# Loading attention keys in 8 KB rows, with transposes that sort two interleaved batches

## The chip, the cores and the metric

One core of one Trainium2 chip. Times are device microseconds of whole executions. The medians are of unprofiled runs; a profile is one more execution, a little shorter or longer. All profiled runs here are fast, with a mean granted TensorE clock of 0.98 to 0.99 of full speed. Ratios are the mean time of one kernel's fast runs over that of the kernel before in the same rounds, so not quite the ratio of the medians that are quoted beside them.

## The reference, cut to what matters

Two independent attention blocks A and B, bf16, whose outputs are put side by side:

```python
B, Sq, D = 16, 64, 640;  H, Sk, Dh = 32, 512, 128
q = (x @ wq).reshape(B, Sq, H, Dh).transpose(0, 2, 1, 3)
scores = einsum("bhqd,bhkd->bhqk", q, k_cache) * Dh ** -0.5
p = softmax(scores)
o = einsum("bhqk,bhkd->bhqd", p, v_cache)
out = o.transpose(0, 2, 1, 3).reshape(B, Sq, H * Dh) @ wo
```

The two K and two V caches are 67 MB each and every byte is used once, so 268 MB of the 295 MB moved are K and V.

## The kernel before

The work is cut into 128 **packs** of two batches and four heads. In each pack TensorE projects the queries (QP), computes the scores (S), transposes the probabilities (TR), multiplies them with V (PV) and applies `wo` (OP). ScalarE takes the exponentials (EX) with row sums. VectorE transposes K (KT), copies the transposed probabilities out of PSUM (TE), takes reciprocals of the row sums (RC) and, once in four packs, moves the output sum (OS). GpSimd scales the probabilities (NM). The kernel gives each engine one ordered list. The lists are sorted by planned times, in packs: `OS=2.53` of pack n-2 falls at the same time as the first RC, 0.53, of pack n, and stands ahead of it.

A pack's K arrives as two DMAs, one per batch, of 128 rows of 4 KB: partition 32·head + p holds 16 keys. VectorE then transposes blocks of 32 x 32 fp32 words (each word two bf16 values of one key), so that keys end up along the free dimension:

```python
def em_LDK(e, op):                      # one batch b of pack n
    src = blocks[blk][1][2 * bp + b, h:h + 4].rearrange("h (p t) d -> (h p) (t d)", t=16)
    ins = e.dma_start(kn_ring[:, n % NK, b, :], src)
...
def em_KT(e, op):
    dst = kt_ring[:, n % NKT, b].rearrange("p t j k two -> p (t j k two)").bitcast(F32)
    ins = e.transpose(dst, kn_ring[:, n % NK, b, :].bitcast(F32))
...
def em_S(e, op):                        # 32 matmuls a pack
    last = e.matmul(ps[64 * b:64 * b + 64, i, :], qs_ring[rows, n % NQ, f, b, :],
                    kt_ring[rows, n % NKT, b, :, f // 2, :, f % 2],
                    start=(f == 0), stop=(f == 3), tile_position=(32 * i, 64 * b))
...
def exp_views(h):                       # every fourth pack ("narrow") reorders keys for its V layout
    if h // 4 % NJ in WIDE:
        return src, dst
    return (src.rearrange("q (th tl k) -> q tl k th", th=2, tl=8), ...)
```

The rings hold six packs of K and four of V. SyncE issues the loads in a fixed order as slots become free.

## Time and profile before

| | before |
|---|---|
| median | 757.96 us (757.82 to 759.49, 3 runs) |
| span of the profiled run | 757.4 us |
| DMA | 295.12 MB, full in all slices but the first and the last two |
| TensorE busy | 90% (98% from 60 to 225 us and from 640 to 738 us) |
| VectorE busy | 71% |
| one transpose of 1024 columns | 1236 ns, 256 of them |
| score matmuls of a pack | 146.4 us / 128 = 1.14 us |

Read it in two steps. The slices show which resources are full on average, here DMA and nearly TensorE. The windows and the waits then show which one holds up the other in each stretch. The lines are in the prediction below. Two groups are needed for the comparison with the profile after (line, engine, operation, tiles, shapes, count; then busy us, mean ns; then idle time before them and what ended it):

```profile
L610 DVE STREAM_TRANSPOSE kt_ring<-kn_ring 128x1024 f32<-128x1024 f32 x256 | 313.6, 1236 | 105.8 <-DMA kn_ring<-in_B_k_cache_dram 70.3
...
L620 PE MATMUL ps<-kt_ring,qs_ring 32*64 32x512 bf16 x4096 | 146.4, 396 | 0.0
```

VectorE had 106 us of idle time ahead of its transposes, most of it waiting for keys to land.

### The profile page before, as it was taken

The numbers are of one execution on the slowest core, as the hardware profiler recorded it, in microseconds if no ns is written. First come the engines' busy times: TensorE is split into PE (matmuls) and PEld (weight loads), VectorE is DVE, ScalarE is ACT, GpSimd is POOL, SyncE is SP. The second block draws the span as 40 slices with busy tenths as digits, with TensorE's granted clock in tenths as the row PEclk, the third lists the DMA queues.
The fourth block names the chain that finished last, engine by engine and source line by source line (L and its number), as shares of the span: only waits on it lengthen the run. The fifth ranks groups of instructions, "written<-read, shape, count | busy, mean of one in ns | idle before, by whom it ended". The sixth has DMA issues, their size and how long they took to land.

```text
span 757.4 us, 57362 instructions
## 1 busy us (share of the span) xinstructions
PE 682.2 (90%) x26518; PEld 528.0 (70%) x26518; DVE 536.7 (71%) x818; ACT 519.6 (69%) x1559; POOL 404.6 (53%) x580
## 2 busy tenths in 40 slices
PE   4579999999999989999978999899997999999995
PEld 3457777777777767777756776677775777777773
DVE  7437777877767777687756777777675787887873
ACT  2437777777777677767756777777775677777772
POOL 5434555546864544645674455445486556455550
PEclk9979999999999999999999999999999999999997
DMA  8999999999999999999999999999999999999970
GB/s 309 394 399 405 406 406 407 406 405 407 400 395 409 407 408 406 407 407 407 406 394 401 406 407 407 406 405 405 406 403 395 406 408 407 402 409 406 407 294 16
DMA packets 99804, 295.12 MB, mean 390 GB/s; under 512 B 9264, under 2 KB 24112, under 8 KB 99760
## 3 DMA queue, kind: packets, MB, share of 16 engines
q1 hardware_dynamic: 91120, 284.20, 95.7%
q10 hardware_dynamic: 8640, 10.49, 3.8%
q14 instruction: 35, 0.29, 0.1%
q8 instruction: 9, 0.15, 0.1%
HBM read 292.03 MB, written 2.62 MB: 389 GB/s over the span
## 4 chain that ended last, share of the span: by engine, by line
PE 33%; SPq 26%; DMA 19%; POOL 9%; DVE 8%; issue 5%; ACT 0%; POOLq 0%; DVEq 0%; ACTq 0%
SPq L546 12%; POOL pn_sb L670 8%; SPq L557 8%; PE ps L705 8%; PE ps L725 8%; PE ps L597 7%; DMA kn_ring<-in_B_k_cache_dram 6%; PE ps L620 6%; DMA kn_ring<-in_A_k_cache_dram 5%; PE ps L681 5%; SPq L559 5%; DMA v_ring<-in_B_v_cache_dram 5%; DVE pT_sb L691 3%; DMA v_ring<-in_A_v_cache_dram 3%; DVE kt_ring L610 1%
## 5 line engine op out<-in xcount | busy, mean ns | idle before, releaser
L670 POOL TENSOR_SCALAR pn_sb<-p_ring,recip 128x512 bf16<-128x512 bf16 x508 | 342.3, 694 | 322.9 <-DVE recip L654 322.8
L610 DVE STREAM_TRANSPOSE kt_ring<-kn_ring 128x1024 f32<-128x1024 f32 x256 | 313.6, 1236 | 105.8 <-DMA kn_ring<-in_B_k_cache_dram 70.3
L641 ACT ACTIVATE p_ring<-ps 128x512 bf16<-128x512 f32 x512 | 298.7, 598 | 32.1 <-PE ps L620 20.3
L691 DVE COPY pT_sb<-ps 128x1024 bf16<-128x1024 bf16 x258 | 164.6, 679 | 79.5 <-PE ps L681 78.8
L705 PE MATMUL ps<-pT_sb,v_ring 32*128 32x64 bf16 (+1 forms) x14528 | 156.7, 192 | 26.2 <-DMA v_ring<-in_B_v_cache_dram 11.0
L725 PE MATMUL ps<-wo_sb,oT_sb 128*128 128x320 bf16 x1040 | 166.6, 303 | 5.9 <-issue 4.8
L597 PE MATMUL ps<-xT_ring,wqp_sb 128*128 128x128 bf16 x2560 | 166.0, 220 | 6.1 <-POOL xT_ring L586 5.8
L705 PEld LDWEIGHTS ps<-pT_sb,v_ring 32*128 32x128 bf16 (+1 forms) x14528 | 142.1, 92 | 40.6 <-DMA v_ring<-in_B_v_cache_dram 14.1
L597 PEld LDWEIGHTS ps<-xT_ring,wqp_sb 128*128 128x128 bf16 x2560 | 157.4, 114 | 13.0 <-issue 6.0
L713 ACT ACTIVATE oT_sb<-ps 128x256 bf16<-128x256 f32 x260 | 85.6, 381 | 107.0 <-PE ps L705 107.0
L620 PE MATMUL ps<-kt_ring,qs_ring 32*64 32x512 bf16 x4096 | 146.4, 396 | 0.0
L603 ACT ACTIVATE qs_ring<-ps 128x512 bf16<-128x512 f32 x128 | 76.5, 598 | 87.7 <-PE ps L597 87.6
L681 PEld LDWEIGHTS ps<-ident,pn_sb 64*128 64x128 bf16 x4128 | 70.8, 95 | 86.8 <-ACT ps L717 65.6
L725 PEld LDWEIGHTS ps<-wo_sb,oT_sb 128*128 128x128 bf16 x1040 | 91.9, 98 | 43.8 <-issue 5.4
L681 PE MATMUL ps<-ident,pn_sb 64*128 64x64 bf16 x4128 | 84.0, 191 | 26.4 <-POOL pn_sb L670 19.8
L641 ACT ACTIVATION_READ_ACCUMULATOR p_ring<-ps 128x1 f32 x512 | 105.9, 207 | 0.0
L620 PEld LDWEIGHTS ps<-kt_ring,qs_ring 32*64 32x64 bf16 x4096 | 55.1, 104 | 31.3 <-issue 0.5
L654 DVE RECIPROCAL recip<-rowsum 128x3 f32<-128x3 f32 (+1 forms) x256 | 36.1, 158 | 24.5 <-ACT p_ring L641 21.2
L717 ACT ACTIVATE ps<-zeros 128x256 f32<-128x256 bf16 x130 | 51.3, 395 | 0.0
L569 POOL COPY wqp_sb<-ws_sb 128x1280 bf16<-128x1280 bf16 x32 | 39.3, 1260 | 7.5 <-DMA ws_sb<-in_A_wq_dram 7.5
L586 POOL COPY xT_ring<-xs_sb 128x640 bf16<-128x640 bf16 x32 | 23.0, 720 | 3.6 <-PE ps L597 3.6
L576 PE MATMUL ps<-ident,xn_ring 128*128 128x128 bf16 x165 | 14.9, 222 | 4.7 <-DMA xn_ring<-in_A_x_dram 3.5
(26 smaller groups left out, 66.3 us busy)
## 6 DMA issues: line engine op xcount, KB each, us to landing
kn_ring<-in_A_k_cache_dram SPq DMA_DIRECT2D x128, 512.0 KB, 14.1
v_ring<-in_A_v_cache_dram SPq DMA_DIRECT2D x128, 512.0 KB, 13.0
kn_ring<-in_B_k_cache_dram SPq DMA_DIRECT2D x128, 512.0 KB, 15.1
v_ring<-in_B_v_cache_dram SPq DMA_DIRECT2D x128, 512.0 KB, 12.7
ws_sb<-in_B_wq_dram SPq DMA_DIRECT2D x10, 512.0 KB, 15.6
wo_sb<-in_B_wo_dram ACTq DMA_DIRECT2D x8, 640.0 KB, 10.9
ws_sb<-in_A_wq_dram SPq DMA_DIRECT2D x4, 640.0 KB, 10.1
wo_sb<-in_A_wo_dram SPq DMA_DIRECT2D x4, 640.0 KB, 12.5
```

What stands on the lines that cost most here:

```text
L546: ins = e.dma_start(kn_ring[:, n % NK, b, :], src)
L597: last = e.matmul(ps[:, 1, f * 128:(f + 1) * 128], w[:, kt, f, :], xT_ring[:, xs, kt, :], start=(kt == 0), stop=(kt == KT - 1))
L603: ins = e.activation(qs_ring[:, op.idx % NQ].rearrange("p f b q -> p (f b q)"), ps[:, 1, :], ACTF.Copy, scale=scale)
L610: ins = e.transpose(dst, kn_ring[:, n % NK, b, :].bitcast(F32))
L620: last = e.matmul(ps[64 * b:64 * b + 64, i, :], qs_ring[rows, n % NQ, f, b, :], kt_ring[rows, n % NKT, b, :, f // 2, :, f % 2], start=(f = ...
L641: ins = e.activation(dst, src, ACTF.Exp, scale=1.0, accum_out=rowsum[:, h:h + 1])
L670: ins = e.tensor_scalar(dst, src, recip[:, h // 4 % NR, i:i + 1], 1.0, ALU.mult, ALU.mult)
L681: last = e.transpose(pt_bank(b)[:, 64 * c:64 * c + 64], pn_sb[rows, c, :], ident[rows, rows], tile_position=(64 * b, 0))
L691: ins = e.tensor_copy(pT_sb[:, b].rearrange("p t q -> p (t q)"), pt_bank(b))
L705: last = e.matmul(ps[:, 4 + i, 64 * b:64 * b + 64], v_ring[rows, n % NV, b, c, :], pT_sb[rows, b, c, :], start=(t == 0 and i < 2), stop=(t ...
L713: ins = e.activation(oT_sb[:, 2 * a:2 * a + 2, :], o_ps[:, 2 * a:2 * a + 2, :], ACTF.Copy)
L725: last = e.matmul(out_ps[:, s, :], oT_sb[:, i, :], wo_sb[:, 4 * j + i, s * NH0:(s + 1) * NH0], start=(j == 0 and i == 0), stop=(j == NJ - ...
```

## The change

The intent is to halve the number of K packets and so to spend less DMA time on the part of each that does not scale with its size (12.2 ns, by the mean 87.9 and 163.6 ns that 2 and 4 KB packets take in the trace of the kernel before). A batch's four heads are only 64 rows of 8 KB, so the two batches of a pack are laid on even and odd partitions. A transposed block then has the keys of both batches alternating; the transposes are given an output pattern that separates them again (16 words of one batch, then 16 of the other). The exponentials undo the new key order. Apart from that the reciprocal is put ahead of the output sum. The planned time of a pack's second load is also changed, but it only serves to work out dependencies: the loads are sorted by another key. The diff is cut to what matters (`...`).

```diff
-  OE=(2.0, 2.06), ZO=2.11, OP=2.31, OS=2.53, ...
+  OE=(2.0, 2.06), ZO=2.11, OP=2.31, OS=2.545, ...
-            add("dve", "KT", (n, b), tk, [("kn", n % cfg.NK, b)], ...)
+            add("dve", "KT", (n, b), tk, [("kn", n % cfg.NK, 0), ("kn", n % cfg.NK, 1)], ...)
-            op = add("sp", "LDK", (n, b), tk - 0.9, ...)
+            op = add("sp", "LDK", (n, b), n + AT["KT"][0] - 0.9, ...)
-        kt_ring = sb("kt_ring", [128, NKT, 2, 16, 2, 32, 2], BF16)
+        kt_ring = sb("kt_ring", [128, NKT, 32, 2, 2, 16, 2], BF16)
 def em_LDK
-            src = ....rearrange("h (p t) d -> (h p) (t d)", t=16)
-            ins = e.dma_start(kn_ring[:, n % NK, b, :], src)
+            src = ....rearrange("h (p t) d -> (h p) (t d)", t=32)
+            dst = kn_ring[b::2, n % NK].rearrange("p a c -> p (a c)")
+            ins = e.dma_start(dst, src)
 def em_KT
-            dst = kt_ring[:, n % NKT, b].rearrange("p t j k two -> p (t j k two)").bitcast(F32)
-            ins = e.transpose(dst, kn_ring[:, n % NK, b, :].bitcast(F32))
+            dst = kt_ring[:, n % NKT, 16 * a:16 * a + 16].rearrange("p t j b k two -> p (t j) b (k two)").bitcast(F32)
+            ins = e.transpose(dst.rearrange("p c b k -> p c k b"),
+                              kn_ring[:, n % NK, a, :].bitcast(F32).rearrange("p (c k b) -> p c k b", k=16, b=2))
 def em_S
-                                        kt_ring[rows, n % NKT, b, :, f // 2, :, f % 2],
+                                        kt_ring[rows, n % NKT, :, f // 2, b, :, f % 2],
 def exp_views
+            u = 2 if h // 4 % NJ in WIDE else 4
+            return (src.rearrange("q (u t p) -> q t p u", u=u, p=16), dst.rearrange("q (t p u) -> q t p u", p=16, u=u))
```

More of the change, by code (lines that the diff above doesn't have):

```diff
@@ L32 @@
               EX=(0.21, 0.32, 0.43, 0.54), RC=(0.53, 0.75), NM=(0.56, 0.69, 0.82, 0.95), NMZ=(0.54, 0.55, 0.56, 0.76), TR=1.2,
-              TE=(1.26, 1.39), PV=1.75, OE=(2.0, 2.06), ZO=2.11, OP=2.31, OS=2.53, LDWO=2.6, ST=3.374, WP0=-1.75, WP1=-1.6)
+              TE=(1.26, 1.39), PV=1.75, OE=(2.0, 2.06), ZO=2.11, OP=2.31, OS=2.545, LDWO=2.6, ST=3.374, WP0=-1.75, WP1=-1.6)
 class Op:
@@ L143, in build_plan @@
             tk = n + AT["KT"][b]
-            add("dve", "KT", (n, b), tk, [("kn", n % cfg.NK, b)], [("kt", n % cfg.NKT, b)])
-            op = add("sp", "LDK", (n, b), tk - 0.9, [], [("kn", n % cfg.NK, b)])
+            add("dve", "KT", (n, b), tk, [("kn", n % cfg.NK, 0), ("kn", n % cfg.NK, 1)], [("kt", n % cfg.NKT, b)])
+            op = add("sp", "LDK", (n, b), n + AT["KT"][0] - 0.9, [], [("kn", n % cfg.NK, b)])
             loads.append((n - cfg.NV + AT["PV"] + 0.2 - cfg.KLEAD, 2, op))
@@ L544, in em_LDK @@
             blk, bp, j, h = pack_info(n)
-            src = blocks[blk][1][2 * bp + b, h:h + 4].rearrange("h (p t) d -> (h p) (t d)", t=16)
-            ins = e.dma_start(kn_ring[:, n % NK, b, :], src)
+            src = blocks[blk][1][2 * bp + b, h:h + 4].rearrange("h (p t) d -> (h p) (t d)", t=32)
+            dst = kn_ring[b::2, n % NK].rearrange("p a c -> p (a c)")
+            ins = e.dma_start(dst, src)
             return ins, ins
@@ L607, in em_KT @@
         def em_KT(e, op):
-            n, b = op.idx
-            dst = kt_ring[:, n % NKT, b].rearrange("p t j k two -> p (t j k two)").bitcast(F32)
-            ins = e.transpose(dst, kn_ring[:, n % NK, b, :].bitcast(F32))
+            n, a = op.idx
+            dst = kt_ring[:, n % NKT, 16 * a:16 * a + 16].rearrange("p t j b k two -> p (t j) b (k two)").bitcast(F32)
+            ins = e.transpose(dst.rearrange("p c b k -> p c k b"),
+                              kn_ring[:, n % NK, a, :].bitcast(F32).rearrange("p (c k b) -> p c k b", k=16, b=2))
             return ins, ins
@@ L632, in exp_views @@
             src, dst = ps[:, h % 4, :], p_ring[:, h % NP, :]
-            if h // 4 % NJ in WIDE:
-                return src, dst
-            return (src.rearrange("q (th tl k) -> q tl k th", th=2, tl=8),
-                    dst.rearrange("q (tl k th) -> q tl k th", tl=8, th=2))
+            u = 2 if h // 4 % NJ in WIDE else 4
+            return (src.rearrange("q (u t p) -> q t p u", u=u, p=16), dst.rearrange("q (t p u) -> q t p u", p=16, u=u))
         def em_EX(e, op):
```

## The prediction

> **What bounds the kernel now.** I read the page's totals first, then the DMA part, then the windows, then the waits of the DMA queue and of the engines, and last the timeline of one stretch.
>
> The page's totals and slices:
>
> ```profile
> span 757.4 us, 57362 instructions
> PE 682.2 (90%) x26518; PEld 528.0 (70%) x26518; DVE 536.7 (71%) x818; ACT 519.6 (69%) x1559; POOL 404.6 (53%) x580
> ...
> DMA  8999999999999999999999999999999999999970
> ...
> DMA packets 99804, 295.12 MB, mean 390 GB/s; under 512 B 9264, under 2 KB 24112, under 8 KB 99760
> ```
>
> The DMA engines are full in every slice but the first and the last, and TensorE is at 90%. Either could be the bound, so the windows must say where each is. Columns: PE, PEld, DVE, ACT, POOL busy, granted clock, DMA share, GB/s.
>
> ```profile
> 60.00:225.00 165.00, 161.72 (x6466) 126.36 (x6458) 123.97 (x194) 126.73 (x379) 99.17 (x142) 1.00 1.03 404
> 225.00:640.00 415.00, 378.82 (x14861) 292.97 (x14851) 298.69 (x454) 292.03 (x880) 226.11 (x324) 1.00 1.03 405
> 640.00:738.00 98.00, 95.63 (x3785) 74.87 (x3784) 76.59 (x116) 72.79 (x221) 52.67 (x79) 1.00 0.98 386
> ```
>
> The DMA share is 1.03 in the first two (packets overlap by 3%, so 1.03 means full). But TensorE is 98% busy in the first and third stretch and 91% in the middle. The waits tell them apart. From 60 to 225 us the DMA queue itself waits for ring slots that the PV matmuls free:
>
> ```profile
> SPq L557 <- PE ps L705: 35.9, 20, 3.3
> SPq L559 <- PE ps L705: 22.5, 8, 3.3
> ```
>
> These 58 us in 165 mean that loads are held back by compute. From 225 to 640 us the same two lines sum to 13 us in 415, and VectorE waits for keys instead:
>
> ```profile
> DVE kt_ring L610 <- DMA kn_ring<-in_B_k_cache_dram: 66.3, 55, 3.9
> DVE kt_ring L610 <- DMA kn_ring<-in_A_k_cache_dram: 31.3, 34, 2.4
> ```
>
> So the kernel is balanced on two limits. A pack is one pair of batches and four heads, 128 in all, four loads of 512 KB each. TensorE bounds the packs from 60 to 225 us and from 640 us on: the score matmuls start 5.09, 5.48, 5.44 and 5.09 us apart, 21.1 us for four packs. DMA bounds the 415 us in the middle, where the weights of the next phases come on top and four packs take some 22.7 us (73 packs in 415 us, by the 2336 score matmuls of that window at 32 a pack).
>
> [...]
> - [...] grouping its packet records by size, 2048 B take 87.9 ns in the mean (16,384 of them) and 4096 B 163.6 ns (59,264). The difference, 75.7 ns for 2048 B, leaves 12.2 ns that do not scale. With the tenth percentiles (84 and 159) it is 9 ns.
> - [...] Every large load of the kernel before fills 128 partitions, so its trace shows nothing of every other partition.
> - [...] 1236 ns for 1024 fp32 columns[...].
> - [...] the exponentials of every fourth pack already read pairs 256 columns apart and take 598 ns, the others, contiguous, 597 ns.
>
> **The change, part by part.**
>
> 1. *K in 8 KB rows.* K is 256 DMAs of 128 packets of 4 KB, 32,768 packets; it becomes 16,384 of 8 KB. By the line through 2 and 4 KB, 8192 B should take 163.6 + 2 x 75.7 = 315 ns against 2 x 163.6 = 327: 9 to 12 ns saved per 8 KB. Times 16,384 over 16 engines is 9.2 to 12.5 us, 9 to 12 with the 3% overlap, or 0.07 to 0.095 us a pack. This counts only where DMA is the bound: 73 packs x 0.08 = 6 us. In the 49 packs or so under TensorE it makes slack, no time.
>
> 2. *Interleaved partitions.* Same bytes[...]. I count nothing for it; it is a rival below. Each transpose now needs both halves of a pack: the first starts about 1.3 us later after its own half (512 KB at 405 GB/s). In the TensorE stretches keys wait for VectorE, and in the middle the queue is never empty, so I count 0.
>
> 3. *Transposes that write in another order.* Still two per pack, 1024 columns each, the source contiguous. Only the write changes: neighbouring results now go 64 B apart. I take it as 1236 ns again. There is room if not: in the TensorE stretch the pair ran from 112.29 to 114.64 us and the next copies could not start before 115.69.
>
> ```profile
> 112.29 2.35 DVE L610 STREAM_TRANSPOSE kt_ring<-kn_ring 128x1024 f32<-128x1024 f32 x2
> ...
> 115.69 1.29 DVE L691 COPY pT_sb<-ps 128x1024 bf16<-128x1024 bf16 x2 [1.04 <-PE ps L681]
> ```
>
> So about 1 us per pack, over 40% on the pair, is free.
>
> 4. *Score matmuls* read runs of 16 keys instead of 32, the step inside a run (4 B) unchanged. The step is what I expect to matter: no change from 1.14 us a pack.
>
> 5. *Exponentials* all read PSUM in pairs or fours with a step. By the 598 against 597 ns above, no change.
>
> 6. *Reciprocal ahead of the output sum.* Once in four packs VectorE does the 0.81 us sum first, and the reciprocal and with it GpSimd's scaling start 0.7 us later. TensorE feels only the last bit of that:
>
> ```profile
> 106.06 0.81 DVE L735 COPY acc<-ps 128x640 f32<-128x640 f32 x1
> 106.80 0.22 DVE L654 RECIPROCAL recip<-rowsum 128x3 f32<-128x3 f32 x2
> ...
> 109.90 0.64 PE L681 MATMUL ps<-ident,pn_sb 64*128 64x64 bf16 x32 [0.27 <-POOL pn_sb L670]
> ```
>
> 0.27 to 0.34 us per four packs. There are about 12 such groups in the TensorE stretches: 3 to 4 us, of which I take 2.5 to 3, since the sum now ends nearer to the PV matmuls that need its PSUM bank. In the middle it only adds slack.
>
> Sum: 6 + 2.5 to 3 = about 9 us; 758 - 9 = **749 us**, 1.2% faster.
>
> **The rivals.**
> - [...] nothing in the trace tells how such rows are dealt out. [...] If K moved 10% slower, its 134 MB, some 330 us of DMA time, would add 33 us, minus what TensorE's stretches hide: 770 to 790 us.
> - *The strided write slows the transposes.* [...] Under +40% nothing much happens; at double, VectorE needs 2 x 2.47 + 1.29 + 0.33 + 0.2 = 6.8 us a pack and becomes the bound: near 900 us.
> - *Shorter runs slow the score matmuls.* Each 0.1 us a pack costs about 5 us in the TensorE stretches; at +0.5 us TensorE becomes the bound everywhere (5.8 us a pack): 790 us.
> - *DMA is the bound throughout.* The TensorE stretches run at 404 GB/s, nearly the rate of the middle, so the limits there may coincide. With the reciprocal moved as well, all of 12 us and 3 us more could show: 743 us. This is the way to a gain of 2%.
>
> **Range and chances.** The expected effects lie between -5 and -15 us, all but the last within 2% (742.8 us). The two bad rivals that could exceed 2% (773 us) have about 15% together, with part of the upper range for their mild forms. So 749, from 741 to 766; faster 0.14, same 0.71, slower 0.15.
>
> **What would show it.** Right: 8192 B packets of 312 to 318 ns; transposes still near 1236 ns; score matmuls still 1.14 us a pack; exponentials near 598 ns; in the first TensorE stretch four packs in about 20.85 us instead of 21.1, and the idle time before the pn transposes there gone; VectorE's waits for keys in the middle somewhat smaller. Wrong: 8 KB packets at 330 ns or more or fewer GB/s in the middle[...], transposes over 1.7 us (write), or a gain above 15 us (then DMA bounded the TensorE stretches too).

What was stated there without a trace of this case is cut and the places are marked: rules about the layout of on-chip memory and about VectorE, how the rows of a load are dealt to the DMA engines, and the reasons drawn from these for and against the first two rivals. The first rival is that K moves slower when each load fills every second partition. The 1236 ns for 1024 columns are those of one transpose. The sum is 6 us for the packets and 2.5 to 3 us for the reciprocal. The zeros for the partitions and for the transposes were estimates; the trace of the kernel before showed neither a load to every second partition nor a transpose with another output pattern.

## The result, and the profile after

752.58 us median (752.36 to 752.85, 4 runs) against 758.35 us in the same rounds; ratio 0.9922, 95% interval 0.9905 to 0.9939. So 0.8% faster, within the 2% that counts as the same, and 3.6 us above the predicted 749.

The page's totals and DMA line of the kernel after:

```profile
span 751.1 us, 57490 instructions
PE 677.3 (90%) x26518; PEld 528.9 (70%) x26518; DVE 677.6 (90%) x818; ACT 520.8 (69%) x1559; POOL 404.9 (54%) x580
...
DMA packets 83421, 295.13 MB, mean 393 GB/s; under 512 B 9264, under 2 KB 24112, under 8 KB 66992
```

The same bytes went in 16,383 packets fewer. But VectorE, at the same 818 instructions, rose from 536.7 to 677.6 us. The two groups that answer to those shown of before:

```profile
L611 DVE STREAM_TRANSPOSE kt_ring<-kn_ring 128x1024 f32<-128x1024 f32 x256 | 478.7, 1948 | 24.3 <-DMA kn_ring<-in_B_k_cache_dram 20.6
...
L622 PE MATMUL ps<-kt_ring,qs_ring 32*64 32x512 bf16 x4096 | 139.1, 383 | 0.0
```

A transpose takes 1948 ns instead of 1236, and the score matmuls 139.1 / 128 = 1.09 us a pack instead of 1.14. The windows (PE, PEld, DVE, ACT, POOL busy, granted clock, DMA share, GB/s):

```profile
60.00:225.00 165.00, 159.13 (x6350) 124.91 (x6348) 160.78 (x195) 126.74 (x381) 98.44 (x140) 1.00 1.03 409
225.00:640.00 415.00, 384.94 (x15168) 301.43 (x15167) 383.91 (x464) 299.48 (x900) 230.66 (x330) 1.00 1.03 411
```

In the first stretch VectorE is now 97% busy, and TensorE has fallen from 98% to 96%. In the middle the loads run at 411 GB/s instead of 405. The waits of the DMA queue say the same (engine and line that waited, on whom: total us, times, longest), first from 60 to 225 us and then from 225 to 640 us:

```profile
SPq L558 <- PE ps L705: 70.0, 23, 3.7
SPq L560 <- PE ps L705: 23.7, 8, 3.6
...
SPq L560 <- PE ps L705: 37.8, 18, 3.4
SPq L558 <- PE ps L705: 37.0, 25, 3.4
```

SyncE, which issues the loads, now waits for free ring slots for 94 us instead of 58 in the first stretch, and for 75 us instead of 13 in the middle. This does not mean that the DMA engines stood idle. Their share is 1.03 in both stretches, and by the packet records fewer than 16 packets were in flight for at most 0.1% of either stretch, before and after: the issued loads form a queue (medians of 8 to 17 us from issue to landing), and it never ran dry there. So the DMA engines run on at full rate, and where compute sets the pace they get ahead. When pack 37 starts, 93.3 MB have landed in the kernel after and 91.2 MB in the kernel before. The chain of waits shows what sets the pace of the first stretch now, in order of time (start, us, what) for one part of it:

```profile
103.98 3.75 DVE kt_ring L611 x2
107.73 1.11 DVE pT_sb L691 x2
...
109.69 3.63 DVE kt_ring L611 x2
113.32 1.11 DVE pT_sb L691 x2
...
114.60 2.71 POOL pn_sb L670 x4
```

The pairs of transposes, which before lay in VectorE's spare time (the same view of the kernel before, from 100 to 125 us, names none), are now on the path: copies of the probabilities start right when the transposes end, and the next reciprocal and the scaling follow late.

From the start times of each pack's first score matmul in the traces (packs counted from 0), with two experiments of the next section beside them:

| start of pack (us) | 0 | 5 | 33 | 37 | 109 | 127 | span |
|---|---|---|---|---|---|---|---|
| before | 15.4 | 60.7 | 209.0 | 230.8 | 642.3 | 738.4 | 757.4 |
| after | 16.7 | 62.7 | 212.0 | 233.0 | 636.6 | 732.3 | 751.1 |
| rows4k | 16.7 | 61.5 | 210.9 | 233.0 | 644.6 | 740.2 | 761.5 |
| rc_first_before | 15.4 | 60.2 | 206.9 | 231.1 | 641.8 | 737.7 | 757.1 |

The kernel after is 2.2 us behind at pack 37, and gains nearly all it gains between packs 37 and 109: 403.5 us instead of 411.5.

### The profile page after: what moved, and what is told of

It is laid out like the page before. It is cut to its first block, busy times and chain, and to the rows that moved or that the text cites. A ratio compares the mean times of both kernels' runs of the same rounds, so it can differ in the third digit from the quotient of the medians.

```text
span 751.1 us, 57490 instructions
## 1 busy us (share of the span) xinstructions
PE 677.3 (90%) x26518; PEld 528.9 (70%) x26518; DVE 677.6 (90%) x818; ACT 520.8 (69%) x1559; POOL 404.9 (54%) x580
## 4 chain that ended last, share of the span: by engine, by line
DVE 32%; PE 21%; DMA 17%; POOL 9%; SPq 9%; issue 6%; ACT 5%; ACTq 0%; DVEq 0%
DVE kt_ring L611 22%; DMA kn_ring<-in_B_k_cache_dram 11%; POOL pn_sb L670 9%; DVE pT_sb L691 6%; DMA kn_ring<-in_A_k_cache_dram 6%; PE ps L705 5%; PE ps L725 5%; ACT p_ring L641 5%; PE ps L598 5%; SPq L547 4%; SPq L560 3%; PE ps L681 3%; PE ps L622 3%; SPq L558 1%; DVE recip L654 1%
## 5 line engine op out<-in xcount | busy, mean ns | idle before, releaser
L611 DVE STREAM_TRANSPOSE kt_ring<-kn_ring 128x1024 f32<-128x1024 f32 x256 | 478.7, 1948 | 24.3 <-DMA kn_ring<-in_B_k_cache_dram 20.6
L705 PEld LDWEIGHTS ps<-pT_sb,v_ring 32*128 32x128 bf16 (+1 forms) x14528 | 143.8, 92 | 38.6 <-issue 29.6
L622 PE MATMUL ps<-kt_ring,qs_ring 32*64 32x512 bf16 x4096 | 139.1, 383 | 0.0
L622 PEld LDWEIGHTS ps<-kt_ring,qs_ring 32*64 32x64 bf16 x4096 | 53.2, 104 | 29.0 <-issue 1.2
L654 DVE RECIPROCAL recip<-rowsum 128x3 f32<-128x3 f32 (+1 forms) x256 | 39.6, 160 | 13.8 <-ACT p_ring L641 11.0
## 6 DMA issues: line engine op xcount, KB each, us to landing
kn_ring<-in_A_k_cache_dram SPq DMA_DIRECT2D x128, 512.0 KB, 12.2
```

The source lines that it names most:

```text
L611: ins = e.transpose(dst.rearrange("p c b k -> p c k b"), kn_ring[:, n % NK, a, :].bitcast(F32).rearrange("p (c k b) -> p c k b", k=16, b=2))
L705: last = e.matmul(ps[:, 4 + i, 64 * b:64 * b + 64], v_ring[rows, n % NV, b, c, :], pT_sb[rows, b, c, :], start=(t == 0 and i < 2), stop=(t ...
```

## The experiments

All were timed beside the kernel before, and all passed the comparison with the reference. So did rows4k, whose keys are in a wrong order on purpose: presumably because the probabilities are nearly uniform for inputs this small. The comparison says little about the order of keys, which in the other variants rests on the derivation of their layouts. "Groups of g" below means that within a transposed block g keys of one batch stand side by side, then g of the other: the changed kernel has g = 16.

| run | what differs from the kernel after | median us | before | ratio (95%) |
|---|---|---|---|---|
| after_again | nothing | 753.13 | 759.44 | 0.9912 (0.9896 to 0.9928) |
| rows4k | K in 4 KB rows | 762.18 | 758.76 | 1.0039 (1.0022 to 1.0056) |
| g1_dense | g = 1, dense write | 820.78 | 758.76 | 1.082 (1.0806 to 1.0834) |
| g2_pairs | g = 2 | 820.39 | 758.76 | 1.082 (1.0806 to 1.0835) |
| g4_quads | g = 4 | 755.96 | 758.76 | 0.9959 (0.9945 to 0.9972) |
| g8_octets | g = 8 | 754.52 | 759.32 | 0.9942 (0.9928 to 0.9956) |
| far | batches 4 KB apart | 755.19 | 759.32 | 0.9948 (0.9935 to 0.9960) |
| os_first | output sum first again | 754.33 | 759.32 | 0.9936 (0.9919 to 0.9952) |
| rc_merged | one reciprocal a pack | 757.15 | 759.32 | 0.9975 (0.9959 to 0.9991) |
| early_pt | two memsets earlier | 753.51 | 759.44 | 0.9930 (0.9915 to 0.9945) |
| rc_first_before | (kernel before) reciprocal first | 757.69 | 759.07 | 0.9979 (0.9960 to 0.9997) |
| mixed | (kernel before) 8 KB rows in the middle only | 755.39 | 759.07 | 0.9946 (0.9926 to 0.9965) |

My theory after reading the traces: the 8 KB packets brought what they promised, and the transposes' scattered write took part of it back by making VectorE the bound where DMA is not. The rivals: the gain comes from the score matmuls or the reciprocal; the slower transposes cost nothing; or what slows them is the shape of the pattern rather than where it writes.

### What the 8 KB rows are worth: rows4k

```diff
-            src = ....rearrange("h (p t) d -> (h p) (t d)", t=32)
-            dst = kn_ring[b::2, n % NK].rearrange("p a c -> p (a c)")
-            ins = e.dma_start(dst, src)
+            src = ....rearrange("h (p t) d -> (h p) (t d)", t=16)
+            ins = e.dma_start(kn_ring[:, n % NK, b, :], src)
```

> The changed kernel with K again in 4 KB rows on all 128 partitions, everything else (strided transposes, both halves awaited, reciprocal first) kept; the result is wrong on purpose. Theory (8 KB packets saved 11.7 us of DMA time, nearly all of which shows where DMA is the bound): 4 KB packets at 163.6 ns, 405 GB/s in the middle, and the time goes up by 8 to 11 us to about 761 to 764 us, slower than the kernel before, since the slow transposes stay. Rival (the gain came from elsewhere, such as faster score matmuls or the reciprocal): time stays within 2 us of 752.5.

762.18 us, ratio 1.0039. The difference of the two ratios to the kernel before, 1.0039 - 0.9922 = 0.0117, is 8.9 us (9.6 us with the 0.9912 of after_again). The first and the middle window of rows4k, to be compared with the 409 and 411 GB/s above:

```profile
60.00:225.00 165.00, 159.15 (x6349) 124.84 (x6347) 161.07 (x194) 126.53 (x380) 98.42 (x140) 1.00 1.03 404
225.00:640.00 415.00, 374.43 (x14933) 292.76 (x14939) 375.56 (x453) 291.00 (x874) 227.70 (x326) 1.00 1.03 405
```

The packet records of the traces, grouped by size, give 163.7 ns for 4096 B here and 315.6 ns for 8192 B in the kernel after. So by the ratios 8 KB rows are worth about 9 us, and all that the change does besides them costs about 3 us (ratio 1.0039, of which the interval excludes 1). The start times in the table say a little less: rows4k and the kernel after are at the same time at pack 37, 8.0 us apart at pack 109 and 7.9 at pack 127. The profiled spans differ by 10.4 us, because rows4k takes 21.3 us from there to its end instead of 18.8, at a granted clock of 0.66 instead of 0.92: its last eight matmuls take 2.33 us instead of 1.27. By then all keys and values have landed, so this part goes with the clock and not with the packets.

The packet records also show where the 8.0 us come from. At pack 37 both kernels are at 233.0 us, but 93.3 MB have landed in the kernel after and 92.0 MB in rows4k. From there to pack 109 it moves 165.7 MB at 410.7 GB/s, rows4k 166.8 MB at 405.1. The rate makes 5.6 us of the difference, and the load lead, 1.3 MB at pack 37 and 0.3 MB at pack 109, the other 2.5.

In the first stretch rows4k and the kernel after both take 21.34 us for four packs, although the loads run at 404 GB/s in one and 409 in the other. So the loads do not set the pace there, and the rival that DMA bounds everything falls.

One more comparison isolates the rest of the change. rows4k and rc_first_before both have 4 KB rows and the reciprocal first. They differ in the transposes with their new layout and in the wait for both halves. rows4k needs 21.34 us for four packs of the first stretch instead of 20.96, and starts pack 127 2.5 us later.

### Why the transposes are slow, and what it would take to make them fast: groups of 1, 2, 4, 8, and far

The edit for a group size g:

```diff
-        kt_ring = sb("kt_ring", [128, NKT, 32, 2, 2, 16, 2], BF16)
+        kt_ring = sb("kt_ring", [128, NKT, 32, 2, 16 // g, 2, g, 2], BF16)
-   dst ....rearrange("p t j b k two -> p (t j) b (k two)") ...  src ...rearrange("p (c k b) -> p c k b", k=16, b=2)
+   dst ....rearrange("p t j m b k two -> p (t j m) b (k two)") ...  src ...rearrange("p (c k b) -> p c k b", k=g, b=2)
-   kt_ring[rows, n % NKT, :, f // 2, b, :, f % 2]
+   kt_ring[rows, n % NKT, :, f // 2, :, b, :, f % 2]
```

> The changed kernel with transposes that write densely (both batches' keys alternate, 4 B apart) and score matmuls that read every second pair (8 B step instead of 4 B). Theory (the jump of 64 B between neighbouring writes slowed the transposes from 1236 to 1948 ns and ate the rest of the gain): transposes back at 1236 ns, VectorE back near 75% in the stretch from 60 to 225 us. If the score matmuls stay at 1.07 to 1.14 us a pack: first score matmul back at 15.4 us (-1.3 us), four packs in about 20.8 us in the TensorE stretches, in all about 745 us. Rival (the step of the key reads is what TensorE feels): score matmuls slower than 1.14 us, by 0.2 us a pack or more; then TensorE is over 98% busy and the time is 752 us or more although VectorE is free. Rival (the slower transposes cost nothing in the end): 752.5 us with transposes at 1236 ns.

> The changed kernel, with the two batches' keys alternating in groups of two: the transpose's write pattern keeps its three dimensions with an innermost count of 2, but neighbouring writes go 8 B apart within 16 B. Theory that the distance of the write matters: 1236 ns, at most 1300. Rival that the shape of the pattern (innermost run of two elements) costs: 1948 ns as in the changed kernel. The score matmuls read two keys, then skip two[...].

> The same with groups of four: neighbouring writes 16 B apart[...]. Theory [...]: 1948 ns as in the changed kernel. Rival that only longer distances (64 B) cost: 1236 ns. Score matmuls between 1.07 and 1.14 us a pack either way. If the transposes are fast, about 745 us; if slow, about 752.5.

> Groups of eight: neighbouring writes 32 B apart[...]. Theory ([...] whatever the distance): transposes between the 2045 ns of groups of four and the 1948 of sixteen, score matmuls 1.07 to 1.09 us a pack, 752.5 to 756 us. Rival (distance matters): a value outside that span.

For "far" the ring is `[128, NKT, 2, 32, 2, 16, 2]`: one area for each batch.

> The changed kernel with the two batches' keys in two separate areas, so that neighbouring writes of a transpose go 4 KB apart instead of 64 B; the score matmuls read the same runs of 16 keys, 128 B apart instead of 256. Theory ([...] the distance does not matter): transposes 1.85 to 2.05 us, time 751 to 756. Rival (the cost grows with the distance): over 2.2 us, VectorE the bound, over 775 us. Rival [...]: near 1.22 us and about 745 us.

The cuts in the last four of these texts are reasons given for the numbers that no run had shown, or that stood without their number. The expected numbers are all kept.

Measured:

| | neighbouring writes apart | ns of a transpose | a matmul's keys lie | score matmuls, us a pack |
|---|---|---|---|---|
| before | 4 B | 1236 | 32 in a run, 4 B apart; batches 4 KB apart | 1.14 |
| g = 1 | 4 B | 1221 | every 8 B | 2.01 |
| g = 2 | 8 B, within 16 B | 1221 | 2, then 8 B left out | 2.01 |
| g = 4 | 16 B | 2045 | 4, then 16 B left out | 1.08 |
| g = 8 | 32 B | 2016 | 8, then 32 B left out | 1.09 |
| g = 16 (after) | 64 B | 1948 | 16, then 192 B left out | 1.09 |
| far | 4 KB | 2017 | 16, then 64 B left out; batches 4 KB apart | 1.16 |

For g = 1 to 8 the pattern given holds within 128 B; the next 128 B, which belong to other matmuls, are left out as well.

The two groups of g = 2 and of g = 4, on either side of the step:

```profile
L611 DVE STREAM_TRANSPOSE kt_ring<-kn_ring 128x1024 f32<-128x1024 f32 x256 | 302.9, 1221 | 1.0 <-DMA kn_ring<-in_A_k_cache_dram 1.0
L622 PE MATMUL ps<-kt_ring,qs_ring 32*64 32x512 bf16 x4096 | 257.0, 618 | 0.0
```

```profile
L611 DVE STREAM_TRANSPOSE kt_ring<-kn_ring 128x1024 f32<-128x1024 f32 x256 | 502.8, 2045 | 14.8 <-DMA kn_ring<-in_B_k_cache_dram 13.4 <-issue 1.4
...
L622 PE MATMUL ps<-kt_ring,qs_ring 32*64 32x512 bf16 x4096 | 138.5, 381 | 0.0
```

Three things follow. First, the pattern's shape is not the cause: g = 2 has the same three dimensions and the same innermost count of 2 as g = 4 and runs as fast as a dense write. Writing alternately to places 16 B or more apart is what costs, and nearly the same from 16 B to 4 KB: 1221 ns at 4 and 8 B, 2045, 2016, 1948 and 2017 ns at 16 B, 32 B, 64 B and 4 KB. Second, the same border appears on the reading side with the sign turned round: the score matmuls take 2.01 us when only two of the keys they want lie in each 16 B, and 1.08 us when all four do. None of the five group sizes passes both. Third, the small speed-up of the score matmuls in the kernel after goes with the nearness of the two batches' keys: 1.08 and 1.09 us a pack with 16 to 64 B between them, 1.14 and 1.16 us with 4 KB. "far" has the same runs of 16 as the kernel after but gives the speed-up back. It also has shorter gaps between its runs (64 instead of 192 B), so that nearness is the cause is likely and not shown, and why it would help is open.

With g = 1 and g = 2 TensorE became the bound (busy for all of the first 165 us window and all of the 415 us in the middle, in both), and the time went to 820 us. The first window of g = 1 has no idle time on TensorE, although VectorE is free for a third of it:

```profile
60.00:225.00 165.00, 165.00 (x5686) 112.54 (x5687) 112.24 (x172) 111.95 (x334) 84.65 (x124) 1.00 0.97 374
```

So the price of dense transposes was higher than the price of scattered ones. My expectation of 745 us for g = 1 was a miss, and the rival noted beside it (the step of the key reads) was right, only far stronger than its 752 us. As for what slow transposes cost in time, g = 4 against g = 16 is a weak test: 97 ns more for each transpose, 0.2 us a pack, and the ratio rises from 0.9922 to 0.9959. In the traces the score matmuls of four packs are 21.74 us apart instead of 21.34 between packs 5 and 33, and no different in the middle (22.4 in both). The other two slow variants lie between: 21.59 us with g = 8 (2016 ns) and 21.68 with far (2017 ns). That fits VectorE's list lying on the path outside the DMA stretch: the eight transposes of four packs take 8 x 97 ns = 0.78 us more, of which half shows.

### The order of the reciprocal: os_first, rc_first_before, rc_merged

```diff
os_first (from the kernel after):          -  OS=2.545   +  OS=2.53
rc_first_before (from the kernel before):  -  OS=2.53    +  OS=2.545
```

> The changed kernel with the output sum ahead of the reciprocal again, as before. Theory (in the changed kernel VectorE is the bound from 60 to 225 us, so the order of two of its instructions moves little, but the scaling on GpSimd starts 0.8 us later once in four packs and TensorE waits for it): four packs 0.1 to 0.4 us longer, in all +1 to +4 us, 753.5 to 756.5. Rival (VectorE's sum of work alone sets the pace, the order is worth nothing): 752.5 within 0.7.

> The kernel before with nothing changed but the order: reciprocal ahead of the output sum. Theory (the prediction's step 6: 0.27 to 0.34 us per four packs in the stretches that TensorE bounds): four packs from 60 to 225 us 20.85 instead of 21.2, in all 755.5 to 757 (2 to 3 us less), ratio 0.996 to 0.998. Rival (the sum now delays the PV matmuls that need its bank, or DMA binds there too): within 1 us of before.

os_first: ratio 0.9936, 1 to 2 us over the kernel after, whose two calls gave 0.9922 and 0.9912; the intervals overlap, so its size is not resolved. Four packs between 5 and 33 took 21.49 us instead of 21.34. rc_first_before: ratio 0.9979, 1.6 us, with an interval that just excludes no effect. Its starts in the table above are the instructive part: it is 2.1 us ahead of the kernel before at pack 33 (four packs in 20.96 instead of 21.19 us) and 0.3 us behind at pack 37. What compute gains ahead of a stretch that waits for loads is taken back there: at pack 37 the same 91.2 MB have landed in both, and between the two packs VectorE's waits for keys rise from 2.5 to 8.0 us. A part may be chance, since the granted clock was halved from 219.5 to 222.9 us in this run and not in the kernel before.

```diff
rc_merged (from the kernel after)
-        for a in range(2):
-            add("dve", "RC", (n, a), n + AT["RC"][a], [("rs", 4 * n + i) for i in ((0, 1, 2), (3,))[a]], ...)
+        add("dve", "RC", (n, 0), n + AT["RC"][0], [("rs", 4 * n + i) for i in range(4)], ...)      # RC=(0.542,)
```

(The scalings of the last pack are moved behind it, from 0.54 to 0.543.)

> The changed kernel with one reciprocal of four sums per pack instead of one of three and one of one. Theory (VectorE is the bound where DMA is not): 0.13 us of VectorE work less per pack, so four packs from 60 to 225 us go from 21.3 to about 20.8 us; with 50 packs outside the DMA stretch 5 to 6 us less, and a little in the middle: 746 to 749 us. Rival (the scaling waits for the fourth exponential now, 0.5 us later, and that latency is what counts): no gain or slower, 752 to 757 us.

A miss: 757.15 us, ratio 0.9975, 4 to 5 us slower than the kernel after. VectorE did less work (156.19 us busy in the first stretch instead of 160.78), yet four packs took 21.96 us instead of 21.34. The timeline of one pack shows the loop that this lengthened:

```profile
115.20 0.18 DVE L652 RECIPROCAL recip<-rowsum 128x4 f32<-128x4 f32 x1 [0.42 <-ACT p_ring L639]
115.47 2.69 POOL L668 TENSOR_SCALAR pn_sb<-p_ring,recip 128x512 bf16<-128x512 bf16 x4 [3.40 <-DVE recip L652]
...
118.31 0.64 PE L679 MATMUL ps<-ident,pn_sb 64*128 64x64 bf16 x32 [0.66 <-POOL pn_sb L668]
```

VectorE stands idle for the fourth exponential, GpSimd for VectorE and TensorE for GpSimd. So it is not VectorE's sum of work alone that binds outside the DMA stretch. The timeline fits a loop through the engines (scores, exponentials, reciprocal, scaling, transposes of the probabilities, and round again) that passes through VectorE's ordered list, and both its length and the work that stands ahead of the reciprocal in that list count.

### A loss in the start: after_again, early_pt

> The changed kernel itself once more, to have it beside the kernel before on the chip of the next run: ratio 0.990 to 0.994.

```diff
early_pt
-            add("dve", "TE", (n, b), n + AT["TE"][b], ...)
+            add("dve", "TE", (n, b), n + AT["TE"][b] if n > -2 else -9.6, ...)
```

> The changed kernel with the two memsets of pT (1.03 us of VectorE, which stood between the first and the second pair of transposes) ahead of the first transposes. Theory (the start is a loss of the slow transposes: 16.7 instead of 15.4 us to the first score matmul, and nothing gives it back before the DMA stretch): first score matmul near 15 us, total 1 to 2 us under the changed kernel of the same call. Rival (the start waits for the loads of the weights anyway): no difference beyond 0.7 us.

The kernel after repeats: 753.13 us, ratio 0.9912. The earlier memsets changed nothing: 753.51 us, and the first score matmul is at 16.7 us as before the edit. The first PV matmuls, which stand ahead of it in TensorE's list, now waited for the first pair of transposes, which the memsets had pushed back by about as much. So the edit did not take the cost away, and whether the 1.3 us of the start reach the end stays open.

### A version made from these: mixed

The kernel before with the reciprocal first. The packs 34 to 105, except every fourth, take 8 KB rows and scattered transposes into the ring layout of before; all others stay as they were.

```diff
+def long_rows(n): return 34 <= n < 106 and n % 4 in Cfg.WIDE
 em_LDK:     +  if long_rows(n): 8 KB rows on every second partition, else as before
 em_KT:      +  if long_rows(n): dst = kt_ring[:, n % NKT, :, :, :, 16*b:16*b+16] ..., written "p c k b", else as before
 exp_views:  +  if long_rows(h // 4): src "q (t u p) -> q t p u" with u=2
```

> 8 KB rows with strided transposes only in the wide packs 34 to 105, where DMA is the bound; 4 KB rows with dense transposes in all others and in every fourth pack; reciprocal first throughout. Theory (8 KB rows pay where DMA binds and slow transposes cost where it does not): first score matmul at 15.4 us, four packs at 21.2 or less from 60 to 180 us as before the change, three quarters of the 8.4 us gained in the middle: 749 to 751 us, 1.0 to 1.2% under before, and 2 to 3 us under the changed kernel. Rival (slow transposes in the starts and ends cost nothing): about 754.5, since a quarter of the packet gain is given up.

755.39 us, ratio 0.9946: better than the kernel before, and no better than the kernel after. The expected 749 to 751 us were missed, and the time is nearer to the rival's 754.5. Its starts: 207.4 us at pack 33 (1.6 us ahead of the kernel before), 234.0 at pack 37 (3.2 us behind), 641.2 at pack 109, 735.3 at pack 127. Between packs 37 and 109 it gained 4.2 us on the kernel before with 52 of 72 packs in 8 KB rows, 0.08 us each. It lost 4.8 us in the four packs where the long rows began. A likely reason is that from there on each pack's keys need both halves and two 2 us transposes (2008 ns each) after landing, which shifts everything once; no run tests it. Up to 1.7 us of the 4.8 may be the granted clock, which was halved for 3.4 us there in this run (an estimate: half of 3.4). None of the variants beats the kernel after.

## Why the prediction was right or wrong

The time, 749 us with 741 to 766, and "within 2%" held. In part this was luck: the packets brought some 2 us more than counted, and the transposes, counted as free, took about as much or more. By its steps:

1. *8 KB packets, right, with its effect put too low.* Predicted 315 ns, measured 315.6. In the trace of the kernel after, 2, 4 and 8 KB take 87.3, 163.2 and 315.6 ns, so some 11 ns do not scale with the size. The saving was counted in the DMA stretch alone, as 6 us; rows4k shows 8.9 to 9.6 us by the ratios, and 8.0 us between packs 37 and 109 by the traces. Of these the higher rate makes 5.6 us, close to the 6 us counted. The part of the estimate that missed is "this counts only where DMA is the bound": the load lead, 1.3 MB more landed than in rows4k by pack 37, gave the other 2.5 us. Behind it stands a misreading: SyncE's 58 us of waiting did not mean that the loads were held back, since the DMA share of 1.03 in the same line of the windows says that the engines stayed full.
2. *Interleaved partitions, right.* Nothing was lost: the middle ran at 411 GB/s with K on every second partition, and at 405 in the kernel before and in rows4k, where K fills all of them. The rival of a K that moves 10% slower falls.
3. *"I take it as 1236 ns again": this is the step that failed.* The transposes took 1948 ns, 58% more. The spare time of about 1 us a pack that the same step had read from the timeline was right and was overrun: the pair grew by 2 x 0.71 = 1.42 us. This is the second rival in a strength between its two cases (nothing up to 40%, near 900 us at double), and one of the prediction's own signs of being wrong, "transposes over 1.7 us". What it cost with the new layout and the wait for both halves, rows4k against rc_first_before shows: 0.38 us for four packs of the first stretch. The reason given against it had no measurement behind it; the one measurement used, exponentials at 598 ns with a step and 597 without, was of another engine and memory: ScalarE reading PSUM.
4. *Score matmuls unchanged: the size was off,* 1.09 instead of 1.14 us a pack, for the better. That the step inside a run matters was the expectation. g = 1, with 8 B instead of 4, took 2.01 us; but g = 2, with the two keys of a run 4 B apart, took 2.01 us as well, so the step alone does not tell.
5. *Exponentials unchanged, right:* 598 ns with the new patterns in all packs.
6. *Reciprocal first, partly.* By itself on the kernel before it brought 1.6 us instead of 2.5 to 3; four packs went to 20.96 us instead of the predicted 20.85. The gain of the first stretch, 2.1 us by pack 33, was lost again by pack 37, which the step had not considered. In the kernel after, four packs take 21.34 us in that stretch, since step 3 overrode it. The waits before the transposes of the probabilities, which were to go, rose there from 2.7 to 4.9 us.

The sum was about -9; measured -5.9 (0.9922 of 758). By the ratios it is made up of -9 for the packets and +3 for everything else together; by the traces up to pack 127, which leave out the end with its lower clock, of -7.9 and +1.8. In everything else the slow transposes, with the wait for both halves, outweigh the reciprocal and the faster score matmuls.

## What to carry to other kernels

A cost that the trace of the kernel before cannot show, here the same instruction with another output pattern (1236 ns before, 1948 after), should get a range rather than its old duration. In this kernel, balanced between loads and compute, relieving one side showed in the stretches that it bounds: 8 KB rows gained 8.0 us between packs 37 and 109, and nothing in the first stretch, where four packs took 21.34 us with either row length. What compute gained ahead of the stretch that waits for loads was taken back inside it (rc_first_before: 2.1 us ahead at pack 33, 0.3 us behind at pack 37); loads that got ahead paid (1.3 MB more landed at pack 37 than in rows4k, 2.5 us by pack 109). Whether loads are held back was to be read from the DMA engines' share (1.03), not from the waits of the engine that issues them (58 us). Layouts have a reader and a writer: here each wanted its own neighbours within 16 B (a transpose 1221 ns with its alternating writes within 16 B, 2045 ns with them 16 B apart; score matmuls 1.08 us a pack with four wanted keys in each 16 B, 2.01 us with two), and the variants that were best for VectorE were the worst for TensorE.
